# Rank product a step later, row numbers and rows of the first expert slot requested and transposed sooner

## Chip, core and metric

One core of one Trainium2 chip runs the kernel. The metric is the device time of one execution in microseconds (us). A profiled execution also leaves a trace; its span runs from the first to the last instruction, and the time of that execution is a little longer than its span.

## What is computed

A linear-attention scan, then a dense two-layer network, then a mixture of eight experts of which each token takes one:

```python
for t in range(S):                                   # B=4, H=8, S=768, D=48
    cur = einsum('bhd,bhe->bhde', u[None] * kt, vt)
    y[:, :, t] = einsum('bhd,bhde->bhe', rt, state + cur)
    state = wt[..., None] * state + einsum('bhd,bhe->bhde', kt, vt)
x = y.transpose(0, 2, 1, 3).reshape(3072, 384)
h = x @ w_in                                         # 384 x 2048
x = (maximum(h, 0) + alpha * minimum(h, 0)) @ w_out  # 2048 x 384
logits = normalise(x) @ normalise(expert_emb).T / tau
expert_idx = argmax(logits); gate_w = softmax(logits)[expert_idx]
for e in range(8):
    out[mask_e] = gate_w[mask_e] * (maximum(x[mask_e] @ w1[e], 0) @ w2[e])
```

## The kernel before

Nothing is scheduled by a compiler: the instructions of each engine stand in the order in which the Python code issues them, and semaphores are added where data or a buffer demands it. Each matrix product is made of three (high part by high part, high by low, low by high).

**Dense part.** The 3072 tokens are 24 tiles of 128; three tiles are a block, and there are eight blocks, 0 to 7. The main loop (line 1025) runs over steps T. A step issues one hidden slice of the first layer of block j = T // 16 (`l1`, line 453, nine matmuls into one of two `h_ps` buffers), then one slice of the second layer, two steps behind (`l2`, line 488, nine matmuls into `o_ps`). ScalarE (ACT) and VectorE (DVE) make the activation of a slice: `m` (lines 463 and 467), its high part `gh` (473) and low part `gl` (478). Ahead of them, at fixed steps, stand the pieces of the attention of later tiles; `2P` and `3P` (lines 341 and 352) transpose a key tile and form products, and take three buffers of the PSUM pool `ps_a`. That pool has three buffers, given out in turn. After block j's last `l2`, `route(j)` (line 505), a Python generator, is resumed once per step (four times per step from T = 112 on) and finds each token's expert. It makes a one-hot `oh` (550) and a running count `carry` (554), pauses for `HOLD` steps (562), multiplies them on TensorE (PE) into `rk_ps` in `ps_a` (565 to 568, the rank product: the token's place among those of its expert), reads that on DVE (570), and turns it into a position `pi` (576). The positions go by GpSimd (POOL), which issues one indirect DMA for each of three tiles, into the table `tbl` in DRAM (584, preceded by a small `spin` fill); the rows themselves go to `x2d` from the SyncE (SP) queue (581).

**Between the parts.** When the counts of blocks 0 to 6 are known, `early_table` (658) works out which expert each of the first five slots has (a slot is 256 tokens of one expert), starting with a PE product of the counts (`totals`, 598). Then `early_loads` (999) issues DMAs from POOL: `pump` loads quarters of expert weights (754, 786 KB each, four to a slot, into four `sg` and two `ld` buffers), `ids_load` (773) reads a slot's token numbers from `tbl`, `gather` (777) fetches 128 rows of `x2d` by those numbers. `EARLY` (66) says at which step, counted from T = 128, a weight quarter's halves are split into high and low part for slot 0 (`split`, 765 and 766) and its rows transposed (`x_T`, 785 to 787).

**Expert part.** The loop at line 1106 runs over steps U. Each has nine matmuls of the first expert layer (`l3`, 796, again into `h_ps`), whose result ACT and DVE turn into `g2h` and `g2l` (800, 801), and six of the second layer two steps behind (`l4`, 822). Splits, transposes, gathers and output of each slot are laid on fixed steps by the table `act`; `pump` is called after each.

Of the kernel before, what the change touches and what calls it, by code (L numbers as in the profile page):

```python
# [45 lines left out]
ES = 5  # L46
# [11 lines left out]
FIRST = [STEPS.index((s, 0)) for s in range(len(KIND))]  # L58
STEP7 = 4
STEP8 = (1, 2, 2, 2, 1)  # L60
HOLD = [1, 1, 2]
ND = range(6)
AD = (0, 1, 3, 4, 5)
WARM0 = 28
WPD = (2, 3)
EARLY = [(0, 0, -5), (0, 1, -5), (0, 2, -4), (0, 3, -3), (1, 0, -1), (1, 1, -1), (0, 4, 0), (0, 5, 0), (0, 6, 1), (0, 7, 1)]
SA = 1
SB = 2
OOB = 1 << 20
# [25 lines left out]
NSG = 4  # L95
# [6 lines left out]
def idx(ap):  # L102
    return bass.IndirectOffsetOnAxis(ap=ap.bitcast(U32), axis=0)
# [3 lines left out]
def tile_main(ctx, tc, keep, x2d, tbl, att, w_in, w_out, alpha, u_row, u_col, emb, tau, w1, w2, cst, out):  # L107
# [383 lines left out]
    state = {"known": ES, "placed": -1}  # L491
# [13 lines left out]
    def route(j):  # L505
# [54 lines left out]
        if j >= NB - 2:  # L560
            bg.append(chain(early_table(), early_loads()) if j == NB - 2 else last_table())
        for _ in range(HOLD[max(j - NB + 3, 0)]):
            yield WAIT
# [28 lines left out]
    xg = []  # L592
# [65 lines left out]
    def early_table():  # L658

        tot = totals(NB - 2, oneb[:, 0:1])  # L660
        nb = above(tot, thr_full, "nb")
        cu = once("cu", [128, 2 * NE])[:, 0:NE]
        DVE.tensor_tensor_scan(cu, nb, nb, 0.0, ALU.add, ALU.bypass)
        DVE.tensor_scalar(out=nb, in0=nb, scalar1=2.0, scalar2=None, op0=ALU.mult)
        yield
        yield from columns(0, ES, at_early, cu, nb, None, None)
        yield
        cm = once("cm", [128, NE])
        DVE.tensor_scalar(out=cm, in0=cu, scalar1=float(ES), scalar2=None, op0=ALU.min)
        DVE.tensor_copy(out=done[:, 0:1], in_=cm[:, 0:1])  # L670
        DVE.tensor_tensor(out=done[:, 1:NE], in0=cm[:, 1:NE], in1=cm[:, 0:NE - 1], op=ALU.subtract)
# [78 lines left out]
    def w_load(s, q):  # L750
        pool, tag = ((sgp, "sg"), (ldp, "ld"))[(4 * s + q) % 3 == 2]
        t = pool.tile([128, WP], F32, tag=tag, name="raw")
        src, h = (w1, w2)[q // 2], q % 2
        POOL.indirect_dma_start(out=t, out_offset=None, in_=src, in_offset=idx(wix[:, h, COL[s]:COL[s] + 1]))  # L754
        raw_t[s, q] = t
# [14 lines left out]
    def ids_load(s):  # L770
        t = sp.tile([128, 2], I32, tag="ids", name="ids", bufs=5)
        n = NTOK[s]
        POOL.indirect_dma_start(out=t[:, 0:n], out_offset=None, in_=tbl.rearrange("(n t) o -> n (t o)", t=n), in_offset=idx(idsx[:, COL[s]:COL[s] + 1]))
        ids_t[s] = t

    def gather(s, t):
        POOL.indirect_dma_start(out=xg[s % 3][:, t, :], out_offset=None, in_=x2d, in_offset=idx(ids_t[s][:, t:t + 1]), bounds_check=NT - 1, oob_is_err=False)
# [90 lines left out]
    if True:  # L868
# [113 lines left out]

        queue = [[divmod(p, 4) for p in range(4 * len(KIND)) if (p % 3 == 2) == i] for i in range(2)]
        busy = [0, 0]
        def pump():
            for i in range(2):
                while queue[i] and busy[i] < (NSG, 2)[i] and queue[i][0][0] < state["known"]:
                    w_load(*queue[i].pop(0))
                    busy[i] += 1

        def split(s, n):
            w_split(s, n)
            if n % 2:
                busy[(4 * s + n // 2) % 3 == 2] -= 1
# [2 lines left out]
            split(s, n)  # L997

        def early_loads():
            pump()  # L1000
            while state["placed"] < NB - 2:
                yield WAIT
            for s in range(ES):
                ids_load(s)
                yield
            for s in range(len(xg)):
                for t in range(2):
                    gather(s, t)
                yield

        def step(k):
            for r in list(bg):
                for _ in range(k):
                    q = next(r, DONE)
                    if q == DONE:
                        bg.remove(r)
                    elif q == DONE_T:
                        state["known"] = len(KIND)
                    if q:
                        break  # L1020
# [4 lines left out]
        for T in range(16 * NB + 2):  # L1025
# [35 lines left out]
            if 32 <= T < 32 + NTILE:  # L1061
                SP.dma_start(out=out[(T - 32) * CH:(T - 31) * CH, :], in_=zero)
            for fn, i, at in EARLY:
                if T - 16 * NB == at:
# [6 lines left out]
        def at(U, fn, *a):  # L1071
            act.setdefault(U, []).append((fn, a))

        for s, k in enumerate(KIND):
            U0, before = FIRST[s], KIND[s - 1]
            at(U0 + (9 if k == "P" else 3), o_scale, s)
            if k == "P":
                for i in range(4 if s else 0):
                    at(U0 + i, split, s, 4 + i)
            else:  # L1080
                for i in range(2):
                    at(U0 + i, relu_single, s, i)
            if s and before == "P":
                for n, i in enumerate((4, 5, 6, 7) if k == "P" else (2, 3, 4, 5, 5, 6, 6, 7)):
                    at(U0 - 8 + i, split, s, n)
            elif s:
                for n in range(4):
                    at(U0 - 2 + (n >= SB), late if n >= SA else split, s, n)
            if s:
                X = U0 - 4 if before == "P" else U0 - 2  # L1090
                for t in range(NTOK[s]):
                    at(X + t, x_T, s, t)
                if s >= ES:
                    at(X - 9, ids_load, s)
                if s >= len(xg):
                    for t in range(NTOK[s]):
                        at(X - 5 + t, gather, s, t)
# [8 lines left out]
        for U in range(n + 3):  # L1106
            first = U - 2 in FIRST
            l34(2, None, l4_single) if first else None
            l34(1, None, turn_single) if first else None
            l34(0, l3, l3_single)  # L1110
            l34(1, None, turn_single) if not first else None
            if U < n:
                l34(2, l4, l4_single if not first else None)
            elif U == n + 1:
                l4_last(len(KIND) - 1, (KE - 2, KE - 1))
            for fn, a in sorted(act.get(U, []), key=lambda e: ORDER.index(e[0].__name__)):
                fn(*a)
            step(STEP8[min(U, len(STEP8) - 1)])
            if U == n - 5:
                POOL.drain()  # L1120
            if not g3[1:] and not bg:
                g3.append(rp.tile([128, KE, CH], F32R, tag="rows", name="g3l"))
            pump()
# [214 lines left out]
@with_exitstack  # L1338
def tile_kernel(ctx, tc, att, w_in, w_out, alpha, u_row, u_col, emb, tau, w1, w2, cst, r, k, v, w, uh, out):
    nc = tc.nc  # L1340
    kp = ctx.enter_context(tc.tile_pool(name="keep", bufs=1))
    dr = ctx.enter_context(tc.tile_pool(name="dram", bufs=1, space=bass.MemoryType.DRAM))
    x2d = dr.tile([NT, ROW], F32, name="x2d")
    tbl = dr.tile([(NE + 1) * NT, 1], I32, name="tbl")
    yd = dr.tile([NT, DM], F32, name="yd")
    ident = kp.tile([128, 128], F32R, name="ident")
    idsx = kp.tile([128, NSLOT], I32, name="idsx")
    wix = kp.tile([128, 2, NSLOT], I32, name="wix")
    cnt = kp.tile([128, 2], I32, name="cnt")
    keep = (ident, idsx, wix, cnt)  # L1350
    with tc.manual_schedule():
        tile_main(tc, keep, x2d, tbl, att, w_in, w_out, alpha, u_row, u_col, emb, tau, w1, w2, cst, out)
        more = nc.values_load(cnt[0:1, 0:1], min_val=0, max_val=128 + NSLOT)  # L1353
        with tc.If(more > 0):
            tile_extra(tc, keep, x2d, w1, w2, out)
            bad = nc.values_load(cnt[0:1, 1:2], min_val=0, max_val=128)
            with tc.If(bad > 0):
                tile_scan(tc, yd, r, k, v, w, uh)
                tile_dense(tc, ident.bitcast(F32), yd, w_in, w_out, alpha, emb, tau, w1, w2, out)
# [57 lines left out]
```

## Time and profile before

| | us |
|---|---|
| median of three runs (811.48 to 814.84) | 813.31 |
| the profiled execution | 813.01 |
| its span | 811.1 |
| PE busy in it | 793.6 |

Times in the rows below are counted from the start of the span. A line of the timeline gives start, duration, engine, source line, operation, output and inputs, shapes, how many were merged into the line and, in brackets, how long the engine was idle before it and what ended that. PE's matmuls overlap, so their pace is the distance between starts, not the duration.

### The profile page before, as it was taken

Reading aid. Unit: us, or ns where it says so; the run is one execution under the profiler, and the core shown is the slowest. Engines: PE = TensorE matmul, PEld = TensorE weight load, DVE = VectorE, ACT = ScalarE, POOL = GpSimd, SP = SyncE. Lnnn points to the kernel's source line nnn. Section 1 sums busy time; section 2 is a strip of 40 time slices with the busy share of each in tenths; the row PEclk is TensorE's granted clock in tenths of the full one; section 3 lists DMA queues with packets and bytes.
Section 4 is the critical chain, followed back from the end, with each engine's and each line's share of the span. In section 5 each row is a group of like instructions: output and inputs, shape, how many; then the busy total and the mean of one; then the engine's idle time right before and its main releaser. Section 6 shows DMA issues by size and latency. Waiting matters only on the chain. (4 is left out here: it accounts for less than half of the span.)

```text
span 811.1 us, 16547 instructions
## 1 busy us (share of the span) xinstructions
PE 793.6 (98%) x6518; PEld 754.8 (93%) x6518; DVE 573.1 (71%) x1167; ACT 440.1 (54%) x885; POOL 302.8 (37%) x365
## 2 busy tenths in 40 slices
PE   9999999999999999999999999999999999999996
PEld 5788899899999999999999999999999999999996
DVE  7989957886666666666766763657797767768662
ACT  5887745445445435444534543336566766767762
POOL 2201122233233233114215212155365777777731
PEclk9999999999999999999999999999999999999999
DMA  9565320345335312122122100085687678776740
GB/s 326 185 212 167 148 70 13 115 60 188 108 98 135 128 30 81 68 83 79 70 89 79 69 32 1 30 231 157 212 199 247 214 250 301 246 257 233 266 157 32
DMA packets 31622, 114.85 MB, mean 142 GB/s; under 512 B 5756, under 2 KB 13148, under 8 KB 29232
## 3 DMA queue, kind: packets, MB, share of 16 engines
q0 software_dynamic: 13952, 59.86, 23.1%
q1 hardware_dynamic: 17584, 53.85, 20.5%
q8 instruction: 53, 0.87, 0.5%
q14 instruction: 33, 0.27, 0.1%
HBM read 99.36 MB, written 15.51 MB: 142 GB/s over the span
## 5 line engine op out<-in xcount | busy, mean ns | idle before, releaser
L463 ACT ACTIVATE m<-h_ps,al_sb 128x384 f32<-128x384 f32 x128 | 74.2, 580 | 135.9 <-PE h_ps L453 129.8
L467 DVE TENSOR_TENSOR m<-h_ps,m 128x384 f32<-128x384 f32 x128 | 70.6, 552 | 95.6 <-ACT m L463 94.0
L473 ACT ACTIVATE gh<-m 128x384 fp32r<-128x384 f32 x128 | 67.2, 526 | 109.6 <-DVE m L467 103.4
L478 DVE TENSOR_TENSOR gl<-m,gh 128x384 fp32r<-128x384 f32 x128 | 78.6, 616 | 34.6 <-ACT gh L473 32.7
L360 POOL TENSOR_SCALAR_AFFINE_SELECT A<-A 128x512 f32<-128x512 f32 x48 | 34.2, 736 | 182.2 <-ACT A L359 182.1
L754 POOL DMA_INDIRECT raw<-in_w,wix x64 | 67.1, 1048 | 52.4 <-DVE w0l L766 32.5
L796 PE MATMUL h_ps<-yh,w0h 128*128 128x256 f32 x264 | 76.7, 291 | 1.7 <-DVE g2l L801 1.4
L796 PE MATMUL h_ps<-yl,w0h 128*128 128x256 f32 x264 | 74.5, 282 | 0.0
L796 PE MATMUL h_ps<-yh,w0l 128*128 128x256 f32 x264 | 74.3, 281 | 0.0
L766 DVE TENSOR_TENSOR w1l<-raw,w1h 128x768 fp32r<-128x768 f32 x64 | 60.4, 953 | 19.4 <-ACT w1h L765 13.9
L766 DVE TENSOR_TENSOR w0l<-raw,w0h 128x768 fp32r<-128x768 f32 x64 | 60.8, 957 | 12.7 <-ACT w0h L765 11.8
L453 PE MATMUL h_ps<-xh,win1h 128*128 128x384 f32 x192 | 68.0, 354 | 1.1 <-DVE m L467 1.1
L453 PE MATMUL h_ps<-xh,win0h 128*128 128x384 f32 x192 | 68.9, 359 | 0.0
L488 PE MATMUL o_ps<-wout0h,gl 128*128 128x392 f32 x192 | 65.5, 341 | 0.5 <-DVE gl L478 0.5
L488 PE MATMUL o_ps<-wout0h,gh 128*128 128x392 f32 x192 | 65.8, 343 | 0.1
L488 PE MATMUL o_ps<-wout1h,gh 128*128 128x392 f32 x192 | 65.7, 342 | 0.0
L453 PE MATMUL h_ps<-xh,win0l 128*128 128x384 f32 x192 | 65.4, 341 | 0.0
L453 PE MATMUL h_ps<-xl,win0h 128*128 128x384 f32 x192 | 65.3, 340 | 0.0
L488 PE MATMUL o_ps<-wout1h,gl 128*128 128x392 f32 x192 | 65.3, 340 | 0.0
L453 PE MATMUL h_ps<-xh,win1l 128*128 128x384 f32 x192 | 65.0, 339 | 0.3 <-DVE win1l L225 0.3
L488 PE MATMUL o_ps<-wout0l,gh 128*128 128x392 f32 x192 | 65.3, 340 | 0.0
L488 PE MATMUL o_ps<-wout1l,gh 128*128 128x392 f32 x192 | 65.2, 339 | 0.0
(284 smaller groups left out, 2267.3 us busy)
## 6 DMA issues: line engine op xcount, KB each, us to landing
ld<-in_att SPq DMA_DIRECT2D x18, 1348.5 KB, 6.0
stg<-in_w_in SPq DMA_DIRECT2D x24, 256.0 KB, 2.9
stg<-in_w_out SPq DMA_DIRECT2D x8, 768.0 KB, 7.5
x2d<-rows SPq DMA_DIRECT2D x24, 194.0 KB, 6.7
out<-zero SPq DMA_DIRECT2D x24, 192.0 KB, 7.0
ld<-in_att SPq DMA_DIRECT2D x5, 512.0 KB, 8.0
ld<-in_att SPq DMA_DIRECT2D x3, 452.5 KB, 6.5
raw<-in_w,wix POOLq DMA_INDIRECT x64
```

The lines of the kernel that those rows point to most:

```text
L360: POOL.affine_select(out=h, in_=h, pattern=[[0, HP], [1, CH]], compare_op=ALU.is_gt, fill=0.0, base=0, channel_multiplier=-1)
L453: PE.matmul(out=h, lhsT=w[:, k, :], rhs=x[:, k, :], start=(n == 0), stop=(n == 3 * KD - 1))
L463: ACT.activation(out=m, in_=h_t[j, f], func=AF.Copy, scale=al_sb[:, f:f + 1])
L467: DVE.tensor_tensor(out=m, in0=h_t.pop((j, f)), in1=m, op=ALU.min)
L473: ACT.activation(out=gh, in_=m_t[j, f], func=AF.Copy)
L478: DVE.tensor_tensor(out=gl, in0=m_t.pop((j, f)), in1=gh.bitcast(F32), op=ALU.subtract)
L488: PE.matmul(out=o_t[j][i], lhsT=g[:, s], rhs=w, start=(f == 0 and n == 0), stop=(f == KF - 1 and n == 2))
L754: POOL.indirect_dma_start(out=t, out_offset=None, in_=src, in_offset=idx(wix[:, h, COL[s]:COL[s] + 1]))
L766: DVE.tensor_tensor(out=lo, in0=a, in1=hi.bitcast(F32), op=ALU.subtract)
L796: PE.matmul(out=h, lhsT=w[:, k, :], rhs=x[:, k, :], start=(n == 0), stop=(n == 3 * KD - 1))
```

## The change

The rank product of blocks 0 to 6 is issued one step later; that of block 7 stays. `early_loads` issues two weight quarters instead of six ahead of the table's use, then the token numbers of three slots (five before), two more quarters, the two gathers of slot 0, the other two quarters, the gathers of slots 1 and 2, and the numbers of slots 3 and 4. The two transposes of slot 0 go from the end of T = 127 to the end of T = 126. Three of the four second-layer splits of slot 0, halves 5 to 7, go from T = 128 and 129 to U = 1, 2 and 3. No instruction is added or taken away.

```diff
-HOLD = [1, 1, 2]
+HOLD = [2, 2, 2]
-EARLY = [(0, 0, -5), (0, 1, -5), (0, 2, -4), (0, 3, -3), (1, 0, -1), (1, 1, -1), (0, 4, 0), (0, 5, 0), (0, 6, 1), (0, 7, 1)]
+EARLY = [(0, 0, -5), (0, 1, -5), (0, 2, -4), (0, 3, -3), (1, 0, -2), (1, 1, -2), (0, 4, 0)]
...
-        def pump():
-            for i in range(2):
-                while queue[i] and busy[i] < (NSG, 2)[i] and queue[i][0][0] < state["known"]:
+        def pump(most=8, of=(0, 1)):
+            for i in of:
+                while most and queue[i] and busy[i] < (NSG, 2)[i] and queue[i][0][0] < state["known"]:
                     w_load(*queue[i].pop(0))
                     busy[i] += 1
+                    most -= 1
...
         def early_loads():
-            pump()
+            pump(2)
             while state["placed"] < NB - 2:
                 yield WAIT
-            for s in range(ES):
+            for s in range(len(xg)):
                 ids_load(s)
-                yield
+            yield
+            for i in (1, 0):
+                pump(1, (i,))
+            yield
             for s in range(len(xg)):
                 for t in range(2):
                     gather(s, t)
                 yield
+                if s == 0:
+                    pump()
+            for s in range(len(xg), ES):
+                ids_load(s)
...
             if k == "P":
-                for i in range(4 if s else 0):
+                for i in range(0 if s else 1, 4):
                     at(U0 + i, split, s, 4 + i)
```

## Rows read from the trace of the kernel before

**Rows 1.** Page, part 1: engine, busy us, share of the span, instructions.

```profile
PE 793.6 (98%) x6518; PEld 754.8 (93%) x6518; DVE 573.1 (71%) x1167; ACT 440.1 (54%) x885; POOL 302.8 (37%) x365
```

**Rows 2.** Waits of PE, whole span: who for whom, us in total, times, longest.

```profile
PE h_ps L796 <- DVE g2l L801: 1.4, 1, 1.4
PE dg_ps L315 <- ACT Kt L344: 1.3, 1, 1.3
PE a_ps L352 <- DVE s_ps L570: 1.2, 3, 0.4
```

**Rows 3.** Timeline of PE: one attention piece unhindered, one behind block 1's rank product.

```profile
165.24 0.60 PE L341 MATMUL kt_ps<-ident,ld 128*128 128x128 f32 x4
...
166.87 0.45 PE L453 MATMUL h_ps<-xh,win1h 128*128 128x384 f32 x1
...
226.28 0.64 PE L341 MATMUL kt_ps<-ident,ld 128*128 128x128 f32 x4
...
228.81 0.44 PE L453 MATMUL h_ps<-xh,win1h 128*128 128x384 f32 x1
```

**Rows 4.** Timeline of DVE at the same two places.

```profile
166.53 0.17 DVE L574 TENSOR_REDUCE s_pf<-s_ps 128x3 f32<-128x24 f32 x1
...
227.50 0.17 DVE L570 TENSOR_TENSOR s_ps<-rk_ps,ebase 128x24 f32<-128x24 f32 x1
```

**Rows 5.** Timeline of POOL and PE in block 3's routing.

```profile
376.90 0.51 POOL L309 TENSOR_TENSOR sbd<-st,PS 48x192 f32<-48x192 f32 x1 [7.09 <-DMA tbl<-tokid,s_pi]
...
386.19 0.35 PE L391 MATMUL y_ps<-sbd,ld 128*64 128x96 f32 x4
```

**Rows 6.** Timeline of PE, then of DVE, at the end of T = 116 and of T = 117.

```profile
518.61 0.34 PE L488 MATMUL o_ps<-wout0h,gl 128*128 128x392 f32 x1
...
520.27 0.42 PE L453 MATMUL h_ps<-xh,win0h 128*128 128x384 f32 x1
...
519.98 0.17 DVE L554 TENSOR_TENSOR carry<-carry,s_ct 128x8 bf16<-128x8 bf16 x1
...
522.80 0.17 DVE L576 CAST s_pi<-s_pf 128x3 int32<-128x3 f32 x1
...
527.54 0.17 DVE L654 TENSOR_SCALAR s_ei<-s_ei 128x5 f32<-128x5 f32 x1
```

**Rows 7.** Timeline of POOL between the parts: table, weights, numbers, rows of slot 0.

```profile
523.25 0.97 POOL L584 DMA_INDIRECT tbl<-tokid,s_pi  x1 [28.15 <-DVE s_tot L601]
...
528.24 0.98 POOL L754 DMA_INDIRECT raw<-in_w,wix  x1 [1.47 <-DVE s_cm L669]
...
535.78 0.95 POOL L773 DMA_INDIRECT ids<-tbl,idsx  x1 [0.30 <-issue]
...
550.11 1.23 POOL L777 DMA_INDIRECT xg<-x2d,ids  x1 [5.80 <-DMA ids<-tbl,idsx]
551.65 1.30 POOL L777 DMA_INDIRECT xg<-x2d,ids  x1 [0.30 <-issue]
```

**Rows 8.** Stretches: us; busy of PE, PEld, DVE, ACT, POOL; clock, DMA share, GB/s.

```profile
530.00:532.00 2.00, 2.00 (x13) 2.00 (x12) 1.15 (x3) 0.78 (x2) 1.43 (x2) 1.00 0.90 18
...
538.00:540.00 2.00, 2.00 (x14) 2.00 (x12) 0.00 (x0) 0.00 (x0) 0.41 (x1) 1.00 1.02 427
```

**Rows 9.** Timeline of PE from the end of T = 126 to U = 2.

```profile
552.19 0.34 PE L453 MATMUL h_ps<-xh,win1h 128*128 128x384 f32 x1
...
555.37 0.82 PE L785 MATMUL x_ps<-ident,xg 128*128 128x128 f32 x6
...
562.92 0.39 PE L796 MATMUL h_ps<-yh,w0h 128*128 128x256 f32 x1 [1.38 <-DVE g2l L801]
```

**Rows 10.** Timeline of DVE, the last splits of slot 0 and the first activation.

```profile
560.71 1.83 DVE L766 TENSOR_TENSOR w1l<-raw,w1h 128x768 fp32r<-128x768 f32 x2 [0.87 <-ACT w1h L765]
562.45 0.75 DVE L801 SCALAR_TENSOR_TENSOR g2l<-h_ps,g2h 128x256 fp32r<-128x256 f32 x2
```

**Rows 11.** Stretches, columns as in rows 8, around the wait at L315.

```profile
40.50:42.00 1.50, 0.36 (x3) 0.03 (x1) 1.50 (x3) 1.50 (x3) 0.00 (x0) 1.00 1.02 398
...
43.50:45.00 1.50, 1.50 (x7) 1.50 (x6) 1.50 (x3) 1.47 (x6) 0.00 (x0) 0.50 0.97 346
45.00:46.50 1.50, 1.50 (x43) 1.06 (x45) 1.47 (x3) 1.50 (x8) 0.00 (x0) 0.50 0.55 206
46.50:48.00 1.50, 1.50 (x31) 1.48 (x24) 1.50 (x3) 1.47 (x5) 0.22 (x1) 0.88 0.06 12
```

## Prediction

> **What bounds the kernel now.** The page's first part gives PE 793.6 us of the 811.1 us span [rows 1], so every other engine matters only where it makes PE wait. I read PE's own waits next: after the start there are few, and three of them belong to the places that the change touches: the attention product at line 352 waiting for the read of a rank product (three times), the expert product at line 796 waiting once for an activation, and a third, at line 315, that the change does not touch but that shows what a wait can do to the clock [rows 2]. Then the timelines around each. So the most that can be won is a few us, and the question is whether the earlier transposes cost as much again.
>
> **Rank product, blocks 1 to 3.** The rank product takes one of three `ps_a` buffers at the end of T = 16j + 26. The next step's attention piece takes three, so its last one must wait until DVE has read the rank product, and DVE does so only after the step's activation work, at 227.50 [rows 4]. Unhindered, the piece takes from 165.24 to 166.87, 1.63 us; behind the rank product from 226.28 to 228.81, 2.53 us [rows 3]. The price is the difference, 0.90 us, more than the 0.4 that the wait itself shows [rows 2]. A step later the rank product comes behind the piece and takes the buffer of `kt`, which ACT has copied out by then; nothing I see takes the place of the wait. Three times 0.90: **2.7 us won**.
>
> **Block 0.** Its attention pieces lie elsewhere in the block: T = 27 has only the transposes of line 409, and T = 28 has the piece that starts at 165.24. The rank product, moved from the end of 26 to the end of 27, now stands directly ahead of a piece that it did not touch before. DVE would read it where the 574 row stands, done near 166.7 [rows 4]; the second product of that piece would otherwise start near 166.0 (165.24, plus 0.15 for the rank product, plus some 0.6 of transposes). **0.8 us lost**, bounds 0 and 0.9 (the price in blocks 1 to 3). Blocks 4 and 5 have no key transposes beside the piece, so three buffers are enough in either order: nothing.
>
> **Block 6.** Here PE loses 520.27 - 518.61 - 0.18 = 1.5 us, first for `oh`, then for `carry` [rows 6]. The rank product leaves this place, but the product of the counts (line 598) stays: `early_table` joins the list of generators before the pause, so it still begins at the end of T = 116. It needs `carry`, written from 519.98 to 520.15 [rows 6], and the next matmul started at 520.27 already. The stall stays; the rank product's own 0.15 us, covered by it until now, comes a step later in the open: **0.1 us lost**, bounds -0.2 (won, if the count product starts a little sooner) and 0.2.
>
> **What is queued behind the later positions.** SP: in blocks 1 to 4 one more row write falls behind a load of attention data; the next to use the row buffer is `o_evac`, over three steps away, so nothing. POOL: the table writes move one step towards or past the state product at line 309. That product sits idle for 7.09 us and the name given is a table write [rows 5]; even a step (3.2 us) later it would be ready, since PE wants it at 386.19, 9.3 us after 376.90 [rows 5]. Nothing, and 0 to 1 us if several such shifts add.
>
> **Splits of slot 0.** At T = 128 and 129 DVE and ACT do four second-layer splits, the transposes' copies and the block's evacuation, and the first `g2l` comes only behind the last pair of splits (from 560.71), at 562.45 [rows 10]. U = 2 needs the `h_ps` buffer that it frees and starts at 562.92 after 1.38 us idle [rows 9]. With three splits gone to U = 1 to 3 (0.9 us of DVE each, half of 1.83 [rows 10], in steps of about 2.1 us that hold little else) and the copies a step earlier, the first `g2l` follows `g2h` at about 560.8 and is done when U = 2 wants it, near 561.4. **1.4 us won**, bounds 0.9 and 1.5. Next late would be the low part of T = 127, which the copies of `x_T` now precede on ACT; I reckon it ready within 0.2 us of its use.
>
> **Transposes a step earlier.** This is the part that can cost. `x_T` for slot 0 goes from 555.37 to 552.19 [rows 9], 3.2 us sooner. The two gathers that it reads were issued at 550.11 and 551.65 [rows 7], so the second took at most 3.7 us to be usable, and there is next to no slack to give away. The gathers must come about 3 us sooner than they did. Do they? On POOL, in the new order:
>
> - Positions: DVE's four instructions on the rank product move behind T = 117's activation, so `pi` is done not at 522.97 but about where the 654 row stands, 527.54 (its predecessors lose as much as they gain) [rows 6]. The first table write follows 0.3 us later, at 527.8. An issue takes 1.26 us of POOL ((535.78 - 528.24) / 6 [rows 7]).
> - Table write 2 at 529.1, weight loads at 530.3 and 531.6, the third table write (it comes in T = 118) at 532.9.
> - The numbers may be read once that third write has landed; call this moment L. Three number reads (3.8 us), two weight loads (2.5) and 0.3 for the gap: first gather at L + 6.6, second at L + 8.1, usable at L + 11.8.
> - PE wants it at 552.45, so PE waits L - 540.65.
>
> L is not in the trace; its bounds are these. In the trace the first number read, issued at 535.78 behind six weight loads, released its gather only at 550.11 [rows 7], when the loads had run through: on POOL's queue a small transfer waits for the bulk ahead of it. The third table write now stands behind two loads. These had a slow opening: issued at 528.24, still 18 GB/s around 531, and 427 GB/s by 538 to 540 [rows 7, 8]. If the opening lasts as long again (full rate from 536.5 before, so from 538.6), two loads of 786 KB end near 541.5 and L is about 542.5. If it does not, they end near 536.4 and L is about 537.7. I take the long opening, because it is the only one of this place that I have. PE then waits **1.9 us**, bounds 0 and 3.
>
> The Trainium skill ("DMA: Bandwidth & Descriptors", section "Queues, rings and completion order") says that each DMA engine consumes a ring in order, and that a semaphore increment lands only after every earlier write of that engine. That speaks against putting the third write behind two loads, and the wait from 535.78 to 550.11 agrees. The same page's fit for one such DMA (2.0 us plus bytes at 436 GB/s; section "Anatomy of one DMA") would end both loads, as an estimate, by 537, and then nothing waits.
>
> **Sum.** Against the profiled execution: 813.01 - 2.7 + 0.8 + 0.1 - 1.4 + 1.9 = 811.7. The median of the runs lies 0.3 above that execution, so 812.0. The later weight quarters (8 and 9 now wait for splits at U = 1 and 3) and slot 1's rows come a few us later than before, yet are first used from U = 4 and later, over 5 us after; nothing.
>
> **Rivals.**
> 1. *The rows are there in time* (L below 541). The sum is then 813.3 - 3.2 = 810.1. For it: two loads instead of six stand ahead. Against: the slow opening.
> 2. *The wait moves to the transposes and grows*: slower. The price is 1 us for each us of L over 540.65, and it passes the 3.2 us won at L = 543.9. If the third table write is held like the number read was, 14.3 us from issue to use [rows 7], L is 547.2 and the wait 6.6 us. A wait of 1.3 us at line 315 was followed by 3 us and more at 0.50 of the clock, the lower of the two levels, 1.2 GHz, where PE had been busy at 1.00 before it [rows 11], which costs about half of 3.4 us, 1.7; the wait of the same length at 562.92 was not [rows 2, 9]. Together 813.3 - 3.2 + 6.6 + 1.7 = 818.4.
> 3. *The same with a middling wait*, 3 to 4 us plus the 1.7 of the clock: 815 to 816.
> 4. *The stalls do not go*: another buffer or another activation makes PE wait at the same places, and the transposes wait little: 813.3.
>
> **How the numbers follow.** Forecast 0.40 (811 to 813.2 by its own bounds), rival 1 0.30, rival 2 0.09, rival 3 0.11, rival 4 0.10. A range from 808.9 (rival 1 without block 0's loss) to 816.0 leaves out rival 2 and little else. Half a per cent, about what a measurement of this kernel can tell from no change, is 4.1 us: faster by more would need all the gains, no new stall in block 0 and no wait, 0.08; slower by more needs rival 2 or the top of rival 3, 0.11; between them 0.81.
>
> **What would show it.** Right: no wait of line 352 on 570 in blocks 1 to 3 and one such in block 0; line 598 still starting near 520.2; no wait of line 796 on 801 near 561; a wait of PE at line 785 on the gather, of one to three us, and the third table write behind two loads on POOL. Wrong: the forecast falls to rival 1 if 785 follows its step without a gap, and to rival 2 if the gap is over 5 us or the clock row beside it reads 0.50.

## The result, and the profile after

The changed kernel takes 816.98 us in the median of seven runs (815.73 to 820.68), the kernel before 813.29 beside it. The ratio is 1.0057, 95% interval 1.0042 to 1.0072: slower by 0.6%, and 1.0 us over the top of the range. The profiled execution took 820.23 us, 3.2 more than that median, so its losses are somewhat larger than the typical ones.

First, where the time went. Three instructions that both kernels have cut the execution into stretches: PE's transposes at line 409 in block 0, the counts' product at line 598, and the same line's second use, in the expert part (starts in us; the last column is PE's last matmul).

```
          line 409   line 598   598 again   last   | stretch 1  stretch 2  stretch 3
before     161.69     520.21     578.58    803.82  |   358.5       58.4      225.2
after      161.44     522.71     585.13    811.18  |   361.3       62.4      226.0
```

Stretch 1 is the rank products of blocks 0 to 5, stretch 2 the way into the expert part. They lost 2.8 and 4.0 us where the prediction's terms sum to -1.9 and +0.6. The page's first part (engine, busy us, share, count) and PE's waits say that the work is the same and the waits are others; they answer to [rows 1, 2]:

```profile
PE 796.0 (97%) x6518; PEld 756.3 (92%) x6518; DVE 568.7 (69%) x1167; ACT 440.6 (54%) x885; POOL 298.2 (36%) x365
...
PE x_ps L785 <- DMA xg<-x2d,ids: 4.6, 2, 3.7
PE t_ps L409 <- DVE y L400: 3.6, 3, 2.4
...
PE tot_ps L598 <- DVE carry L554: 1.3, 1, 1.3
...
PE h_ps L796 <- DVE g2l L801: 0.2, 1, 0.2
```

The three waits of line 352 are gone, and that of line 796 nearly. Two new ones are larger: 3.7 us at the transposes (785), and 2.4 us at line 409.

**The wait at line 409, which nothing had foreseen.** It is in block 1, over 30 us after block 0's rank product. Read from its cause: the timeline of SP, the rows of the DMA issues of 176.15 and 176.53 (count, size, us to landing), then DVE, PE, and stretches (their last three columns: clock, DMA share, GB/s).

```profile
160.21 0.82 SPq L581 DMA_DIRECT2D x2d<-rows  x2
176.15 0.34 SPq L178 DMA_DIRECT2D ld<-in_att  x1
176.53 0.42 SPq L581 DMA_DIRECT2D x2d<-rows  x1
...
ld<-in_att SPq DMA_DIRECT2D x1, 1348.5 KB, 13.4
x2d<-rows SPq DMA_DIRECT2D x1, 194.0 KB, 17.8
...
194.40 0.57 DVE L497 COPY rows<-o_ps 128x392 f32<-128x392 f32 x1 [3.76 <-DMA x2d<-rows]
...
199.33 0.55 PE L409 MATMUL t_ps<-ident,y 128*128 128x128 f32 x3 [2.39 <-DVE y L400]
...
196.00:200.00 4.00, 1.61 (x11) 1.29 (x10) 3.89 (x10) 1.75 (x6) 1.36 (x2) 1.00 0.92 294
200.00:201.00 1.00, 1.00 (x5) 1.00 (x4) 1.00 (x2) 0.67 (x2) 0.00 (x0) 0.50 0.86 305
...
203.00:204.00 1.00, 1.00 (x6) 1.00 (x6) 0.80 (x2) 0.38 (x2) 0.00 (x0) 0.79 0.35 131
```

Before, SP issued block 0's three row writes together, at 160.46. Now the third stands behind a load of attention data. SP issued that load 15 us after the second write (SP's waits put 12.5 us of this to PE's product at line 394, the last reader of the load's buffer) and the third write right behind it, at 176.53. The write landed 17.8 us later, at 194.3, 4.8 us after the load in front of it. That load took 13.4 us; in run 10 below, where no write follows it, it took 13.8, so its slowness is not the change's doing. Block 1's evacuation (line 497) writes the same row buffer and wanted it at 190.6. DVE stood 3.76 us, the scan and the activations queued behind the copy were late, PE stood 2.39 us, and for 3 us and more after that its clock was 0.50, the lower of its two levels (1.2 GHz). In the 4 us before the clock fell, PE had been busy for 1.61.

**Blocks 0 to 3 and 6.** The timeline of PE: block 0's piece, block 1's, and the counts' product, to be set against [rows 3, 6].

```profile
165.00 0.19 PE L565 MATMUL rk_ps<-s_oh,trib 128*128 128x24 bf16 x1
...
165.11 0.63 PE L341 MATMUL kt_ps<-ident,ld 128*128 128x128 f32 x4
165.67 1.68 PE L352 MATMUL a_ps<-ld 64*128 64x128 f32 x16
167.28 0.44 PE L453 MATMUL h_ps<-xh,win1h 128*128 128x384 f32 x1
...
231.66 1.16 PE L352 MATMUL a_ps<-ld 64*128 64x128 f32 x16
...
522.71 0.18 PE L598 MATMUL tot_ps<-carry,oneb 128*128 128x8 bf16 x1 [1.27 <-DVE carry L554]
```

Block 1's piece runs as one row of 16 without a wait. Block 0's takes 2.17 us (165.11 to 167.28) where 1.63 is unhindered. The product of the counts still waits for `carry`.

**The wait at line 785.** POOL, the landing of the gather issued at 552.38, then PE, then the stretches beside it; this answers to [rows 7, 9].

```profile
535.21 1.02 POOL L584 DMA_INDIRECT tbl<-tokid,s_pi  x1 [0.19 <-issue]
544.89 0.97 POOL L773 DMA_INDIRECT ids<-tbl,idsx  x1 [8.66 <-DMA tbl<-tokid,s_pi]
...
552.38 1.26 POOL L777 DMA_INDIRECT xg<-x2d,ids  x1 [0.30 <-issue]
553.95 1.01 POOL L777 DMA_INDIRECT xg<-x2d,ids  x1 [0.31 <-issue]
...
xg<-x2d,ids POOLq DMA_INDIRECT x1, 6.3
...
558.78 1.51 PE L785 MATMUL x_ps<-ident,xg 128*128 128x128 f32 x6 [3.70 <-DMA xg<-x2d,ids]
...
558.00:559.00 1.00, 0.22 (x1) 0.25 (x2) 0.00 (x0) 0.00 (x0) 0.82 (x1) 0.70 0.88 314
559.00:560.00 1.00, 1.00 (x7) 0.98 (x6) 0.00 (x0) 0.31 (x1) 0.88 (x1) 0.50 1.09 350
...
561.00:562.00 1.00, 1.00 (x5) 1.00 (x5) 0.41 (x1) 0.00 (x0) 0.70 (x2) 0.59 0.97 404
```

The third table write is issued at 535.21 and its numbers can be read at 544.89. The row of six transposes begins with three that read the first gather, so this is the gather that PE waits for: it is issued 7.5 us after 544.89 and lands 6.3 us after its issue, at 558.7. The second lands within the next half microsecond, ahead of its use. PE stands 3.70 us, and its clock, 1.00 before the wait, is at 0.50 for about 3 us behind it. The stretch's sum: 1.5 won at the splits, 3.7 to 3.9 lost in the wait, about 1.6 at the clock: 3.9 of the 4.0. These stretches explain the profiled execution, whose span is 7.2 us longer than before. The median of the runs is only 3.7 us longer; which part a typical execution is spared, no profile shows.

### The profile page after: what moved, and what is told of

Read it like the earlier page. It is cut to its first block, busy times and chain, and to the rows that moved or that the text cites. A ratio compares the mean times of both kernels' runs of the same rounds, so it can differ in the third digit from the quotient of the medians.

```text
span 818.3 us, 16545 instructions
## 1 busy us (share of the span) xinstructions
PE 796.0 (97%) x6518; PEld 756.3 (92%) x6518; DVE 568.7 (69%) x1167; ACT 440.6 (54%) x885; POOL 298.2 (36%) x365
## 5 line engine op out<-in xcount | busy, mean ns | idle before, releaser
L478 DVE TENSOR_TENSOR gl<-m,gh 128x384 fp32r<-128x384 f32 x128 | 80.7, 632 | 34.6 <-ACT gh L473 34.5
L766 DVE TENSOR_TENSOR w0l<-raw,w0h 128x768 fp32r<-128x768 f32 x64 | 60.8, 958 | 11.8 <-ACT w0h L765 11.8
```

The lines of the kernel that those rows point to most:

```text
L478: DVE.tensor_tensor(out=gl, in0=m_t.pop((j, f)), in1=gh.bitcast(F32), op=ALU.subtract)
L766: DVE.tensor_tensor(out=lo, in0=a, in1=hi.bitcast(F32), op=ALU.subtract)
```

## The experiments

Theory A: the loss is at the transposes, whose rows come too late. Theory B: the row write behind the load costs as much again. Each kernel was timed beside the kernel before, which took 813.9 to 814.8 us in the median on these chips. So ratios are compared.

**1. Transposes back** (the changed kernel, transposes at the end of T = 127).

```diff
-EARLY = [..., (1, 0, -2), (1, 1, -2), (0, 4, 0)]
+EARLY = [..., (1, 0, -1), (1, 1, -1), (0, 4, 0)]
```

> The changed kernel, only that slot 0's two transposes go back to the end of T = 127. Theory A (the time is lost where PE waits for the gathered rows: in the changed kernel's trace PE came to the transposes at 554.9, the first rows at 558.8, and the clock then fell): PE arrives 3.2 us later, the wait falls from some 4.5 us to about 1.3 and the clock holds, so the time falls by 4 to 5 us from the changed kernel's 817.0 to about 812 to 813. Theory B (the time is lost at the evacuation of block 1, whose buffer waits for a row write, 4.7 us in the changed kernel's trace; the wait at the transposes is only covered slack): no change, 816 to 817.

Measured: 1.0039 (1.0021 to 1.0056). Stretch 1 took 362.4 us, stretch 2 58.7: a good part of stretch 2's loss is gone, stretch 1's is not. PE still waited 1.2 us for the first gather. By the ratios the time fell by 0.2% from the changed kernel's, within the intervals, where theory A had 4 to 5 us.

**2. Block 6's rank product back** (`HOLD = [2, 1, 2]` in the changed kernel).

> The changed kernel, only that block 6's rank product goes back one step (blocks 0 to 5 stay a step later). All three table writes then stand ahead of the first weight load on POOL, as in the kernel before. Theory A with its cause (the third table write sits behind two weight loads): the number reads start near 531 instead of 545, the rows are there by 548, no wait at the transposes, clock at 1.00, and all the gains of the other parts show: 810 to 811. If the cause is instead that the gathers sit behind the next two loads, wherever the table writes stand: PE still waits 2 to 4 us, 813 to 816. Theory B: 816 to 817.

Measured: 1.0007 (0.9991 to 1.0023). Stretch 2 took 57.0 us, with 0.7 us of waits at line 785; stretch 1 360.7, with DVE 4.71 us idle before line 497. Of the versions that put back one part, this is the only one whose interval lies clear below the changed kernel's: about 0.5%, or 4 us.

**3. Rank products of blocks 0 to 5 alone** (`HOLD = [2, 1, 2]` in the kernel before).

> The kernel before, only with the rank products of blocks 0 to 5 a step later; everything between the parts as before. Theory A: 2.7 us won in blocks 1 to 3, 0.5 to 0.8 lost in block 0: 811.1 to 811.4, with single runs about 4 us above that if the row write behind the load lands late as in the changed kernel's profile. Theory B: the row write costs 4.7 us nearly always, 815 to 816.

Measured: 1.0026 (1.0007 to 1.0045). Here nothing of the expert part is changed, and stretch 1 takes 361.6 us, 3.1 more than before. The part of the change that was to win 1.9 us loses by itself.

**4. The splits alone** (the kernel before with three splits at U = 1 to 3).

> The kernel before, only with halves 5 to 7 of slot 0's second-layer splits at U = 1 to 3. Both theories: the wait of 1.4 us at U = 2 goes and nothing takes its place, 811.7 to 812.1. If the wait only moves (to the second-layer products of slot 0, or to a later activation): 813.3.

Measured: 0.9988 (0.9975 to 1.0). Stretch 2 took 56.9 us, 1.5 less than before.

**5. Row writes ahead of the pause** (the changed kernel).

```diff
+        for i in range(nb):
+            ...
+            SP.dma_start(out=x2d[t0:t0 + CH, :], in_=rows[:, i, 0:ROW])
         for _ in range(HOLD[max(j - NB + 3, 0)]):
...
-            SP.dma_start(out=x2d[t0:t0 + CH, :], in_=rows[:, i, 0:ROW])
```

> The changed kernel, but the three row writes of every step are issued on SP's queue ahead of the pause, so none stands behind the next load of attention data; the rank product itself stays where the change put it. Theory B (block 1's evacuation at lines 497 and 499 waits for block 0's third row write, which landed 17.8 us after its issue behind a load; about 4.7 us of PE with the clock beside it): no wait of those lines on a row write, PE at line 409 without the 2.4 us gap near 197, and 816.9 - 4.7 = 812.2. Theory A alone (all of the loss lies in the transposes' wait for the gathers): 816 to 817, the wait at line 785 as before.

Measured: 1.0053 (1.0034 to 1.0072). The mechanism of theory B is shown, its sum is not. SP issues all three writes before the load, DVE and ACT no longer wait at lines 497 and 499, and stretch 1 takes 356.8 us, 4.5 less than in the changed kernel and what the prediction had for it. But stretch 2 took 70.2. The timelines of SP, then ACT and PE (the added lines move the later ones down by three: L789 is the L786 of the other runs):

```profile
159.47 1.31 SPq L565 DMA_DIRECT2D x2d<-rows  x3
160.96 14.93 SPq L178 DMA_DIRECT2D ld<-in_att  x2
...
562.32 0.49 ACT L789 ACTIVATE yh<-x_ps 128x384 fp32r<-128x384 f32 x1 [8.14 <-remote]
...
565.89 0.69 PE L488 MATMUL o_ps<-wout1h,gh 128*128 128x392 f32 x1 [4.66 <-ACT gh L473]
```

PE waited 2.78 us for the rows, and then 4.66 more for ACT, which had stood 8.14 us over a copy of transposed rows that PE had finished at about 553.5. "remote" names no instruction of this core: what held ACT, no record shows.

**6. Block 0's rank product back** (the changed kernel, the pause given for each block; run twice, on two chips).

```diff
-HOLD = [2, 2, 2]
+HOLD = [1, 2, 2, 2, 2, 2, 2, 2]
...
-        for _ in range(HOLD[max(j - NB + 3, 0)]):
+        for _ in range(HOLD[j]):
```

> The changed kernel with only block 0's rank product (and with it its row writes) back at its old step. Theory B: the 4.7 us of the evacuation go, and the 0.5 us in block 0's attention piece with them: 811.7, a little under the run with the row writes alone. Theory A alone: 816.4 (only the 0.5). The wait at line 785 stays at 3 to 4.6 us in both.

> Only block 0 restored, block 6's rank product late: a wait of 3.5 to 4.7 us at line 785 and the clock at 0.50 behind it, 814.5 to 817.5. If block 6's step is not the cause, the same time as the version with both restored.

Measured: 1.0027 (1.0006 to 1.0049) and 1.0035 (1.0017 to 1.0052). In both profiles stretch 1 takes 356.1 us: block 0's delay alone is worth 5.2 us there (its evacuation 4.7, its own piece 0.5). But stretch 2 takes 64.4 and 64.5, 2 us more than in the changed kernel, with PE's clock down twice as long after a wait of the same size. (In the second profile the wait is 4.52 us.) The timeline of PE and a stretch of the first, columns as above:

```profile
552.56 1.51 PE L785 MATMUL x_ps<-ident,xg 128*128 128x128 f32 x6 [3.52 <-DMA xg<-x2d,ids]
...
552.00:558.00 6.00, 5.44 (x19) 5.39 (x20) 1.45 (x3) 1.56 (x3) 4.78 (x5) 0.50 0.92 351
```

**7. Blocks 0 and 6 back** (`HOLD = [1, 2, 2, 2, 2, 2, 1, 2]`; 24 executions on two chips, two single ones on a third).

> The changed kernel with the rank products of block 0 and of block 6 back at their old steps; blocks 1 to 5, the splits and the order of the number reads as in the change. Theories A and B together: no evacuation wait, the wait at line 785 under 1.5 us, so 813.3 - 2.7 (blocks 1 to 3) - 1.3 (splits) + 0 to 1 = 809.3 to 810.3, faster than the kernel before by 0.4 to 0.5%. If the gathers are late by the new order of the number reads and not by block 6's later rank product, 812 to 814.

> The version with blocks 0 and 6 restored once more, for another profile: a time near 810 with a wait at line 785 under 1 us, or a time of 815 to 818 with the transposes waiting 2.5 us or more and the clock at 0.50 behind it (theory: its slow executions are those in which the gathers land late). If a time over 814 shows with no such wait, the theory of the gathers doesn't explain its spread.

> The same kernel again: either of the two, as said for the run before.

> Blocks 0 and 6 restored, the rest of the change kept. If block 6's step is what makes the gathers late: 809.5 to 811, ratio 0.995 to 0.997, most executions close together, and 4 us or more under the version with block 0 alone restored. If a second cost lies in it that the profiles miss: most executions at 814 to 818 again, ratio near 1.

Measured: 1.0000 (0.9974 to 1.0025; 809.57 to 818.15 us), single times of 809.9 and 810.89, and 1.0004 (0.998 to 1.0029; 809.87 to 820.19). Three profiles have 0.5 to 1.2 us of waits at line 785 in the whole span, stretch 1 at 356.0 to 356.2 and stretch 2 at 56.9 to 57.1, and their times are 809.9 to 810.9. POOL's timeline in the first of them shows why the rows are in time:

```profile
524.51 0.97 POOL L584 DMA_INDIRECT tbl<-tokid,s_pi  x1 [0.19 <-issue]
...
533.61 0.96 POOL L773 DMA_INDIRECT ids<-tbl,idsx  x1 [4.50 <-DMA tbl<-tokid,s_pi]
...
542.60 1.01 POOL L777 DMA_INDIRECT xg<-x2d,ids  x1 [0.30 <-issue]
```

The third write comes 10.7 us sooner than in the changed kernel (3.8 of it because PE is that much earlier at line 598), and the gathers 11 us sooner. But of 24 timed executions 17 took over 814 us, and the last profile caught one (span 817.3, stretch 2 63.6, stretch 3 229.2). Its timeline of ACT and PE:

```profile
552.14 0.58 ACT L463 ACTIVATE m<-h_ps,al_sb 128x384 f32<-128x384 f32 x1 [4.71 <-PE x_ps L785]
...
553.37 0.45 PE L453 MATMUL h_ps<-xh,win1h 128*128 128x384 f32 x1 [0.86 <-issue]
...
555.68 0.33 PE L453 MATMUL h_ps<-xh,win1h 128*128 128x384 f32 x1 [1.10 <-issue]
...
557.99 0.58 ACT L463 ACTIVATE m<-h_ps,al_sb 128x384 f32<-128x384 f32 x1 [3.39 <-remote]
...
720.56 0.60 ACT L844 ACTIVATE g3h<-g_ps 128x512 fp32r<-128x512 f32 x1 [3.59 <-remote]
...
721.21 0.44 PE L854 MATMUL o_ps<-w1h,g3h 128*128 128x384 f32 x1 [2.20 <-issue]
```

Just where the transposes now stand, from 551.4 to 556.5, PE moves a matmul or two at a time, and the records name nothing that held it ("issue"). Before 552.14 ACT stood 4.71 us, though the product that it reads was done by about 549.1; its 3.39 us before 557.99 are a wait for PE's late products. The rows were not what was waited for. Nor is this the only place: stretch 3 lost 3 us as well, and there ACT stood 3.59 us before 720.56 over a copy of products that PE had finished by 716.9, and PE then waited 2.20 us for that copy. So my reason for the spread, late gathers, fell; the cause stays open.

**8. Block 6's rank product, the new order and the transposes, without the moved splits** (the kernel before).

> The kernel before with only block 6's rank product a step later, the new order of the number reads and weight loads, and the transposes of the first slot a step sooner; splits and blocks 0 to 5 as before. Theory A (the gathers are late): a wait of 3 to 4.6 us at line 785 and the clock at 0.50 beside it, of which the old wait at line 796 (1.4 us) is covered: 813.3 + 2 to 4 = 815.3 to 817.3. Theory B alone (the evacuation is all of the loss): 813 to 814, since no row write of block 0 moves here.

Measured: 1.0102 (1.0079 to 1.0126), worse than every other. The timelines of PE and ACT:

```profile
557.15 1.51 PE L785 MATMUL x_ps<-ident,xg 128*128 128x128 f32 x6 [3.65 <-DMA xg<-x2d,ids]
...
568.36 0.89 ACT L499 ACTIVATE rows<-o_ps 128x392 f32<-128x392 f32 x2 [4.01 <-PE h_ps L796]
...
572.22 0.58 PE L796 MATMUL h_ps<-yh,w0h 128*128 128x256 f32 x1 [3.26 <-DVE g2l L801]
```

The same wait, and then the old wait of line 796, 3.3 us instead of 1.4. Ahead of it ACT stood 4.01 us before the evacuation at line 499, though PE's last product for it had started at 565.56, and the last splits and `g2l` came only behind that evacuation. No record shows these splits waiting for weights, and none shows what held ACT. The clock falls twice, and stretch 2 takes 69.1 us.

**9. Blocks 1 to 5 and the splits, nothing else** (the kernel before with `HOLD` as in 7 and the splits as in 4), and **10. the same with the new order of loads and numbers** (transposes still at their old step).

> The kernel before with only two parts of the change: rank products of blocks 1 to 5 a step later (block 0 and block 6 at their old steps) and the three splits of slot 0 moved to U = 1 to 3. The order of number reads, weight loads and gathers, and the step of the transposes, are those of before. If the transposes' wait is what takes the gains of these parts back in some executions, it cannot happen here: 813.3 - 2.7 - 1.3 = 809.3, ratio 0.995, and runs close together. If the two gains don't add up, or something else loses in some executions: 812 to 814 with runs up to 818.

> As the run before with the new order of number reads and weight loads as well, the transposes still at their old step. If the step of the transposes is what made block 0 and 6's restored version vary from 809.6 to 818 us, this one stays near 809.5 to 810.5. If the new order alone costs (weights of the first slot split later), 812 to 815 with waits at line 796.

Measured: 0.9961 (0.9947 to 0.9975) and 0.9954 (0.9938 to 0.997), medians 811.61 and 810.08 beside 814.72, and no execution of either over 812.1. Stretch 1 takes 356.8 and 356.0 us, stretch 2 56.9 in both. These two are faster than the kernel before beside them, by 0.4 to 0.5%, and by the ratios faster than the changed kernel by about 1%. Both were timed on one chip only, the one of run 7's two single executions. In 10 the transposes do not wait at all (timeline of PE; then the landing of block 0's first two table writes, issued between 169 and 174 us):

```profile
552.79 0.82 PE L785 MATMUL x_ps<-ident,xg 128*128 128x128 f32 x6
...
tbl<-tokid,s_pi POOLq DMA_INDIRECT x2, 9.1
```

## Why the prediction was wrong

Two steps of the prediction failed. It put the later row writes on SP's queue at nothing and never looked at block 0's, which cost 4.7 us in the profile (point 3). And it put the wait at the transposes at 1.9 us, where it was 3.7 and about 1.6 more at the clock (points 5 and 6).

Stepwise from 10 to the changed kernel, by ratios: 0.9954; with the transposes a step earlier 1.0000 and 1.0004 (about 3.9 us); with block 6's rank product later too, 1.0027 and 1.0035 (2.4 us); with block 0's as well, 1.0057 (2.1 us). The first of these steps and the other two together are clear of the noise; each of the last two alone is not, and the runs were on different chips.

1. **Blocks 1 to 3: right.** 2.7 us forecast; stretch 1 of runs 7 and 10 is 2.3 to 2.6 us shorter (1.8 in run 9), and the waits of line 352 are gone.
2. **Block 0's own piece: right in kind, 0.5 us for 0.8.** It lies within the bounds.
3. **The sentence on SP failed**, and with it the sum. "SP: in blocks 1 to 4 one more row write falls behind a load ...; the next to use the row buffer is `o_evac`, over three steps away, so nothing." For blocks 1 to 4 that held: in run 10 their writes fall behind loads, and lines 497 and 499 wait for none. But block 0 is not in the sentence, and its third write falls behind a load too. Three steps are about 10 us. I had not looked at what that load was waiting for: its own buffer, 15 us more than the write. With 17.8 us to land, the write took 33 us in all, and the evacuation met it. With it stretch 1 is 4 to 6 us longer (runs 1 to 3, and after; 0.5 of it block 0's own piece) than in the runs that move blocks 1 to 5 without it. What it is worth in the time is not settled: 0.53% from 9 to 3 (0.9961, less the 0.9988 of the splits, to 1.0026), 0.2 to 0.3% from 6 to the changed kernel, next to nothing from 7 to 2 (1.0000 and 1.0004 to 1.0007), and nothing from 5, whose stretch 2 gave all of it back.
4. **Block 6: right** that the counts' product keeps its stall (1.27 us). But the step also moved the table writes, and that was priced only through L.
5. **The transposes' wait was mis-sized: 3.7 us for 1.9.** The table's numbers came at 544.89, which with PE's lag of 2.5 us is the forecast 542.5. The reason given for it is not borne out: from its issue to the first read of a number the third write took 9.7 us behind two loads, and 9.1 us ahead of both (run 7). Block 0's first two table writes in run 10 landed 9.1 us after their issue with no weight load on the queue. So L is late because the write is issued late, which the forecast had (532.9 and the lag, for 535.21); that the number came out right is luck. The rule of the Trainium skill that the prediction quotes ("DMA: Bandwidth & Descriptors", section "Queues, rings and completion order": a ring is consumed in order, and a semaphore rises only after the engine's earlier writes) is given there for the queues of SP and ACT; the order in which the two loads and the write behind them landed here agrees with it, 542.2, 544.1 and 544.6. But standing behind the loads was worth only 0.6 us, and over all runs the two orders overlap: 9.4 to 10.1 us behind the loads (runs 1, 5, 6, 8 and after), 8.9 to 9.8 ahead of them (runs 2, 7 and 10).
   L + 11.8 should have been L + 13.9, and it is the first gather that counts: issued 7.5 us after L, not 6.6, and used 6.4 us after its issue. The prediction read the 3.7 us of the second gather from the start of transposes that read the first; by the same rows the first took at most 5.3 us (550.11 to 555.37). Two weight loads stood right ahead of the gathers in the changed kernel, and at 553 to 559 us the DMA engines were moving 309 to 387 GB/s, against 144 to 159 at 552 to 556 before; that this made the gather slower is likely, but no run separates it.
6. **The clock behind the wait** stood in rivals 2 and 3 only. A wait of 3.7 us brought it, as rival 3 had it; that rival, with 3 to 4 us of wait, 1.7 of clock and a chance of 0.11, is what stretch 2 did. Together with point 3 it gives the profiled execution (813.3 - 3.2 + 3.7 + 1.6 + 4.7 = 820.1, for 820.23), 3 us more than the median.
7. **The splits: right.** 1.4 us forecast, 1.5 in stretch 2 of run 4, 1.0 in its time (its stretch 3 was 1.1 longer).
8. **Missing altogether:** run 7's kernel loses time in most executions even when the rows are there in time (3.9 us against 10; the second gather was issued at 542.60, some 8 us before its use). That the transposes' earlier step does it is not shown. On the chip where 10 was timed, both executions of run 7's kernel took 809.9 to 810.9, like 10; the 17 long ones were on two other chips, where 10 was not timed and where the kernel before also had 11 of 47 executions over 816 us, against none of 11. The one profile of a long execution lost about a third of its extra time in stretch 3, far from these transposes. The cause is open.

## What to carry to other kernels

When a DMA issue moves past another on an in-order queue, price the wait of the instruction in front of it (here a buffer that came free 15 us later) and then the landing, and follow the buffer that it reads to its next writer, in every block; a step count is no price. Take the time of a transfer's landing from rows with the same traffic around them, and from the instruction that really reads it. And a change of several parts is best tried part by part: two of these parts win 0.4% together, and with all of them the kernel is 0.6% slower.

## What the hardware showed that I had not expected

A row write of 194 KB took 17.8 us to land behind a load that took 13.4, where the page's median for such writes in the same execution is 3.9. The third table write of block 6 needed 8.9 to 10.1 us before its numbers could be read, loads ahead of it or not, while the two before it landed after 4.1 to 5.8 us where the profiles of runs 7, 10 and after time them; what makes the third slower is open. After waits of 3.5 to 3.7 us the clock stayed at 0.50 for about 3 us in one execution and for 6 in another. And in three profiles (5, 8 and the last of 7) ACT stood 3.6 to 8.1 us over work whose input was ready for most of that time, with nothing shown that held it; all three have the transposes a step earlier, but one of these stops came over 160 us behind them.
